# Three experts with one-hot rows instead of two, weights issued in one run behind the first gathers, page turns moved into the gating chain, a last tile copied by two engines, and a smaller first piece of x

## The chip, the cores and the metric

The kernel runs on one core of a Trainium2 chip. The core has a matmul engine (TensorE, called PE in the profile, with PEld for its weight loads), VectorE (DVE), ScalarE (ACT), GpSimd (POOL) and SyncE (SP). SP, ACT and POOL also issue DMAs, which run on 16 shared DMA engines. Each engine works through its own instructions in order. The metric is the time of one execution on the device in microseconds; the median of several runs counts.

## The reference

The program is a Fourier filter over the sequence, followed by a mixture of experts in which each expert keeps at most 80 tokens:

```python
X = np.fft.rfft(x, axis=1)                  # x: (8, 2496, 256)
y = np.fft.irfft(X * (filt_r + 1j * filt_i), n=2496, axis=1)
x = y.reshape(19968, 256)
logits = x @ w_gate                         # 8 experts
expert = argmax(logits); gate_w = softmax(logits)[expert]
for e in range(8):
    tok = tokens of expert e; at most 80, those with the largest gate_w
    out[tok] = gate_w[tok] * (relu(x[tok] @ w1[e]) @ w2[e])   # 256 -> 1024 -> 256
```

All other rows of the output are zero. So only 640 of the 19968 rows of the inverse transform are ever needed, and the kernel computes only chosen rows of it.

## The kernel before, in words

**Forward transform.** The sequence of 2496 is split as 39 by 64. For each of 16 halves (8 batches, two halves of 128 channels) `stage1` (line 316) multiplies x by a table, ScalarE copies the result, and for each of five groups of frequencies `turn_t` (332) transposes on PE, `stage2` (343) multiplies by the second table, and `filtered` (352) multiplies by the filter on VectorE (line 358) and adds and subtracts on POOL (366). One such group is a step k; the loop at line 1033 has 80 of them. x comes in three chunks per batch by `load_x` (288); the first chunks come in pieces of four rows (`SG`) for each partition.

**Filter.** The filter is read in five groups (`filter_in`, 532), the real part by SP and the imaginary part by POOL, each followed by a part of the second table on SP. `filter_sign` (542, VectorE) changes the sign of some of its rows in place; `filter_turn` (548) then brings a group into place with PE, by plain transposes where the sign has been applied, else by products with a table `perm`, in twice as many passes. There are ten such turns, one ahead of the loop and one in each of the steps 0 to 8. `perms` holds both tables and the signs. Ahead of the loop a row of eight products of zeros keeps PE at work until x lands (line 938).

**Gates.** The logits are found from the spectra, for two batches at a time: `gates` and `turn_z`, `logits`, and `gating` (466) in eleven parts, which leave the best eight candidates per row. For the last batch `gates_last` and `turn_z_last` do this in smaller pieces as the spectrum becomes ready. `threshold` (570) finds by bisection the gate value that keeps 80 tokens of each expert; `mark`, `codes`, `fields`, `row_lists`, `row_index` turn the kept tokens into row numbers.

**Chosen rows of the inverse transform.** The chosen tokens are sorted by batch into seven tiles of 128 rows (`TILES`). For each tile `gather_rows` (895, POOL) reads rows of a table of the inverse transform (640 numbers each), `turn_rows` (906, VectorE) transposes them, and `fill` (913) does the product with the spectrum of the batch, 20 steps per tile. A spectrum as it stands in memory is a page: `load_page` (872) reads it back on SP, and the last batch's page is made on the core by ten calls of `turn_last` (389), each four PE transposes and one ScalarE copy. A finished tile is copied by ScalarE (929) and written to `y_sel` in DRAM by a DMA that ScalarE issues (930).

**Experts.** For an expert its 80 tokens are gathered from `y_sel` by POOL (rows of 256 numbers), transposed (`turn`, 1244), and go through `layer1` (1259), `layer2` (1279), a transposition back (`back`, 1307) and an indirect write to the output (`scatter`, 1317). The first `NH` experts do not wait for the last tile to be written: `last_dg` and `last_hot` (806, 812) make a one-hot matrix `lhot` of the rows that lie in the last tile, the gather at line 1217 reads only the tiles before it, and `turn` adds a product of the last tile, still on the core, with `lhot`. The other experts gather from the whole of `y_sel` (line 1238) and wait for that DMA. `turn(e + 2)` stands between the two halves of `layer2(e)`.

**Weights.** Each expert has two DMAs on SP, `load_first` (w1, 1107) and `load_second` (w2, 1115). They go into places that pages or earlier experts have used: expert 2 takes the place of page 4, 3 that of page 5, 4 that of page 6, 5 to 7 those of experts 0 to 2. With a `mark`, POOL clears one number of the place first, so the DMA is held back until POOL gets there in its queue.

The order of the work on each engine is written out by hand (`tc.manual_schedule()`); from line 1125 on the calls stand in the order in which the engines take them.

## Time and profile before

| | |
|---|---|
| median of 3 runs | 373.41 us (373.08 to 377.3) |
| the profiled execution | 374.22 us |
| its span in the trace | 372.3 us |
| PE busy | 353.7 us, 95% of the span |
| PEld busy | 317.4 us, 85% |
| VectorE busy | 241.2 us, 65% |
| POOL busy | 189.7 us, 51% |
| ScalarE busy | 130.9 us, 35% |
| moved by DMA | 109.96 MB, mean 295 GB/s |

How to read the rows. In a timeline a row is the start, the length, the engine, the line of the kernel, the operation, output <- inputs with their shapes, and the count of instructions merged; in brackets stands the idle time of the engine ahead of it and what ended it. "SPq" and the like are the issuing of DMAs. A list of waits gives the engine and line that waited, what released it, and the sum in us, the number and the longest. In a table of stretches a row is the stretch, its length, the busy time of PE, PEld, DVE, ACT and POOL with the count of instructions, then the granted clock of PE (1.00 is full), the busy share of the DMA engines, and GB/s. A row of a group ends with its busy time, the mean of one in ns, and the idle time ahead of it. The chain of waits is the work that ended last, followed back; its rows are start, length and what. Matmuls are pipelined, so a matmul in f32 appears as passes that overlap, and the spacing of starts says more than the length of one.

### The profile page before, as it was taken

The page shows a single profiled execution, that of the slowest core. Times are in us where ns is not written, and L with a number is a line of the kernel's source. Part 1 is how long each engine was busy: PE and PEld are TensorE (multiplying, and loading weights), DVE is VectorE, ACT ScalarE, POOL GpSimd, SP SyncE. Part 2 cuts the span into 40 slices and gives each one's busy share as a digit, 9 for nine tenths or more (in the row PEclk, how much of TensorE's full clock was granted, in tenths as well). Part 3 has the DMA queues.
Part 4 walks back from the last instruction along what each step waited for, and adds up shares of the span by engine and source line. Part 5 has one row for each costly group of instructions (what it writes and reads, how often), then busy time and mean ns, then how long its engine had stood idle before and what let it go on. Part 6 is the DMA issues. An engine that isn't in the chain of part 4 may idle for free. (4 is left out here: it accounts for less than half of the span.)

```text
span 372.3 us, 9878 instructions
## 1 busy us (share of the span) xinstructions
PE 353.7 (95%) x4021; PEld 317.4 (85%) x4021; DVE 241.2 (65%) x514; ACT 130.9 (35%) x274; POOL 189.7 (51%) x273
## 2 busy tenths in 40 slices
PE   8989999999999999999899999989999999898893
PEld 7989989899899899799699979679886757787793
DVE  6089648748868768979979897688976660111120
ACT  1645454454455455354354444225000000010110
POOL 4688556646646646646457888712275102323111
PEclk9999999999999999999999999999999999899997
DMA  6997659999989999999989979988999966599900
GB/s 229 326 319 271 144 163 297 328 310 321 334 278 337 312 339 355 349 275 339 322 276 291 347 252 325 345 333 325 410 408 407 387 230 227 186 369 369 331 22 26
DMA packets 42235, 109.96 MB, mean 295 GB/s; under 512 B 4533, under 2 KB 14643, under 8 KB 40895
## 3 DMA queue, kind: packets, MB, share of 16 engines
q1 hardware_dynamic: 34708, 83.50, 65.0%
q0 software_dynamic: 6192, 24.60, 19.6%
q10 hardware_dynamic: 1282, 1.14, 1.0%
q8 instruction: 34, 0.56, 0.6%
q14 instruction: 19, 0.16, 0.1%
HBM read 70.44 MB, written 40.37 MB: 298 GB/s over the span
## 5 line engine op out<-in xcount | busy, mean ns | idle before, releaser
L366 POOL TENSOR_TENSOR yt<-p 128x256 f32<-128x256 f32 x159 | 116.5, 755 | 76.3 <-DVE p L358 75.2
L358 DVE TENSOR_TENSOR p<-pb,ft 128x1024 f32<-128x1024 f32 x80 | 97.1, 1215 | 41.9 <-issue 18.2
L323 PE MATMUL pa<-wf_t,x 117*128 117x120 f32 x704 | 92.0, 278 | 0.7 <-DMA x<-in_x_dram 0.7
L323 PEld LDWEIGHTS pa<-wf_t,x 117*128 117x128 f32 x704 | 86.5, 196 | 1.0 <-issue 1.0
L348 PE MATMUL pb<-d_t,t 128*128 128x128 f32 x640 | 84.9, 276 | 0.4 <-DVE p L358 0.3
L348 PEld LDWEIGHTS pb<-d_t,t 128*128 128x128 f32 x640 | 77.8, 192 | 0.9 <-issue 0.8
L328 ACT COPY tt<-pa 128x480 f32<-128x480 f32 x96 | 48.0, 516 | 69.3 <-PE pa L323 68.0
L341 ACT COPY t<-pt 128x512 f32<-128x512 f32 x80 | 47.1, 589 | 16.9 <-PE pt L337 13.8
L379 DVE STREAM_TRANSPOSE u<-yt 128x512 f32<-128x512 f32 x70 | 48.9, 699 | 0.0
L337 PE MATMUL pt<-ident,tt 128*128 128x128 f32 x320 | 48.4, 273 | 0.0
L901 POOL DMA_INDIRECT gt<-rows_tbl,idxr x28 | 29.5, 1053 | 27.3 <-DVE wt L911 19.1
L337 PEld LDWEIGHTS pt<-ident,tt 128*128 128x128 f32 x320 | 37.4, 142 | 1.1 <-issue 1.0
L920 PE MATMUL pr<-page,wt 128*128 128x256 f32 x160 | 36.8, 382 | 0.0
L920 PEld LDWEIGHTS pr<-page,wt 128*128 128x128 f32 x160 | 29.6, 190 | 4.2 <-issue 0.6
L925 PE MATMUL pr<-page,wt 128*32 128x256 f32 x480 | 27.5, 380 | 0.4 <-DVE wt L911 0.4
L911 DVE STREAM_TRANSPOSE wt<-gt 128x640 f32<-128x640 f32 x28 | 21.9, 819 | 5.8 <-DMA gt<-rows_tbl,idxr 5.8
L925 PEld LDWEIGHTS pr<-page,wt 128*32 128x32 f32 x480 | 17.2, 110 | 9.7 <-DVE wt L911 0.9
L1269 PE MATMUL ph_True<-xs_True,w 128*64 128x80 f32 x512 | 21.9, 242 | 2.9 <-issue 2.5
L1318 POOL DMA_INDIRECT out_dram<-ys_True,idxs x8 | 7.5, 932 | 31.6 <-ACT ys_True L1313 22.9
L1269 PEld LDWEIGHTS ph_True<-xs_True,w 128*64 128x64 f32 x512 | 20.2, 144 | 3.9 <-issue 3.8
L929 ACT COPY yr<-pr 128x256 f32<-128x256 f32 x7 | 2.6, 373 | 54.0 <-PE pr L925 28.5
L404 PE MATMUL pz<-yt,wg 128*32 128x512 f32 (+1 forms) x224 | 19.5, 437 | 1.7 <-POOL yt L366 1.7
(220 smaller groups left out, 316.0 us busy)
## 6 DMA issues: line engine op xcount, KB each, us to landing
out_dram<-zero_t SPq DMA_DIRECT2D x32, 624.0 KB
yf<-u SPq DMA_DIRECT2D x56, 320.0 KB
page<-yf SPq DMA_DIRECT2D x14, 1280.0 KB
w<-in_moe_w_dram SPq DMA_DIRECT2D x16, 1024.0 KB
x<-in_x_dram POOLq DMA_DIRECT2D x11, 936.0 KB
x<-in_x_dram SPq DMA_DIRECT2D x12, 468.0 KB
x<-in_x_dram POOLq DMA_DIRECT2D x5, 702.0 KB
fst<-in_filt_r_dram SPq DMA_DIRECT2D x10, 128.0 KB
```

Source lines behind the costliest of these rows:

```text
L323: nc.tensor.matmul(out=ps[:, j, :], rhs=wf_t, start=True, stop=True, lhsT=xt[3 * b + ch][:, j0 + j - JC * ch, 128 * cb:128 * cb + 128])
L328: nc.scalar.copy(out=tt[h][:, :, H3 * j0:H3 * j0 + hn * jn].rearrange("p s (j h) -> p s j h", h=hn), in_=v)
L337: nc.tensor.transpose(ps[:, i, :], tt[h][:, 2 * s:2 * s + 2, :].rearrange("p r n -> p (r n)"), ident[:])
L341: nc.scalar.copy(out=t2[k][:], in_=ps[:])
L348: nc.tensor.matmul(out=ps[:, :, i, :], lhsT=t[:, i, :], rhs=d_t[:, SG * g + i, :], start=True, stop=True)
L358: nc.vector.tensor_tensor(out=p[:], in1=f.unsqueeze(2).to_broadcast(shape), op=AL.mult, in0=ps[:].rearrange("p r s q -> p r (s q)").unsque ...
L366: eng.tensor_tensor(out=y[:, :, 2 * r:2 * r + 2, :], in0=a, in1=b, op=op)
L379: nc.vector.transpose(uu[h][:, :, SG * g:SG * g + SG, :].rearrange("p a s w -> p s a w"), spectrum(h)[:, SG * g:SG * g + SG])
L901: nc.gpsimd.indirect_dma_start(out=gts[t, g][:].rearrange("p s q -> p (s q)"), out_offset=None, in_=quarters, in_offset=bass.IndirectOffse ...
L920: nc.tensor.matmul(st["po"][:], lhsT=wts[t][:, s, :], rhs=columns(pages[t], s), **kw)
L925: nc.tensor.matmul(st["po"][at], lhsT=wts[t][:, s, at], rhs=columns(pages[source(t, g)[0]], s), **kw)
L1269: nc.tensor.matmul(ph[c:c + 64, i, 0:cap], lhsT=w1[:, k, f:f + 64], rhs=xs[:, k, :], start=(k == 0), stop=(k == NDB - 1))
```

## The change

There are five edits. **NH = 3**: a third expert gets one-hot rows; its one-hot product and the second's now stand between steps of the last tile. **Weights**: the second half for expert 3 and both halves for expert 4 are issued right behind those of expert 2, ahead of the last tile's end in the order of the program, and no longer behind the gathers of the other experts; the `mark` for expert 3's second half goes. **Turns**: three of the ten `turn_last` calls move up between the steps that lead to the last logits. **Last tile**: its two halves are copied by ScalarE and VectorE. **Start**: the first chunk of x comes as pieces of 2, 2 and 4 rows and not 4 and 4; ScalarE's DMA for `perms` moves behind the first pieces of stage 1; `filter_sign` moves behind `filtered` in the steps 0 to 4, group 2 (before: ahead of the loop) becomes the last of the five, and so group 2's first turn is by `perm`.

```diff
-NH = 2
+NH = 3
...
             elif i < 7:
-                for j in range(0, jn, SG):
-                    rows_in(0, [(N2, N1), (J3, H3)], r0 + j, min(SG, jn - j), j)
+                cuts = [0, 2, 4, jn] if i == 0 else list(range(0, jn, SG)) + [jn]
+                for j, end in zip(cuts, cuts[1:]):
+                    rows_in(0, [(N2, N1), (J3, H3)], r0 + j, end - j, j)
...
         def last_dg(e):
-            where, tag = ((sp, "bval"), (sp, "spread"))[e]
-            st["dg", e] = where.tile([cap, cap], F32, name=f"dg_{e}", tag=tag)
+            st["dg", e] = sp.tile([cap, cap], F32, name=f"dg_{e}",
+                                  tag=("bval", "spread", "part")[e])
...
-                    nc.scalar.copy(out=yr[:], in_=st["po"][:])
+                    if t < TILES - 1:
+                        nc.scalar.copy(out=yr[:], in_=st["po"][:])
+                    else:
+                        nc.scalar.copy(out=yr[:, 0:128], in_=st["po"][:, 0:128])
+                        nc.vector.tensor_copy(out=yr[:, 128:C], in_=st["po"][:, 128:C])
...
-        nc.scalar.dma_start(out=perms[:], in_=perm_dram.ap())
         for i in range(3):
             load_x(i)
...
         for i in range(4):
             for h in range(2):
                 stage1(h, i)
+            if i == 0:
+                nc.scalar.dma_start(out=perms[:], in_=perm_dram.ap())
...
         next_filter(nc.vector.tensor_copy)
-        filter_sign(2)
...
                 next_filter(nc.scalar.copy)
-                if r < NG - 1:
-                    filter_sign((r + 3) % NG)
...
                 filtered(k, ps)
+            if k < NG:
+                filter_sign((k + 3) % NG)
...
+        pages[B - 1] = keep.tile([128, NS * C], F32, name=f"page_{B - 1}", tag="page1")
         gates_last(2)
...
         gates_last(4)
+        turn_last(0)
         turn_z_last(0, 4)
         fill(1)
         turn_z_last(4, 1)
         gating(2, 8)
+        turn_last(1)
         logits(7, 0)
         for part in range(9, 11):
             gating(2, part)
         fill(1)
+        turn_last(2)
         logits(7, 1)
...
-        pages[B - 1] = keep.tile([128, NS * C], F32, name=f"page_{B - 1}", tag="page1")
         gating(3, 9)
         gating(3, 10)
         threshold(B, cap, 0)
-        for i in range(2 * NG):
+        for i in range(3, 2 * NG):
             turn_last(i)
...
-        last_dg(0)
-        last_dg(1)
+        for e in range(NH):
+            last_dg(e)
...
         last_hot(0)
-        last_hot(1)
         xg = [near_p.tile([cap, C], F32, name=f"xg_first_{e}") for e in range(NH)]
...
         load_first(2, nc.gpsimd.memset)
+        load_first(3)
         load_second(2)
-        load_first(3)
-        fill(20)
+        load_second(3)
+        for e in range(1, NH):
+            fill(2)
+            last_hot(e)
+        fill(22 - 2 * NH)
+        load_weights(4)
...
             gather(e)
-            if first and e == 4:
-                load_second(3, nc.gpsimd.memset)
-                load(4)
```

## The prediction

> **What bounds the kernel now.** I read the page's first lines, then what the matmul engine (PE) waits for, then the end of the run in order of time, where the largest of these waits lies, and last the granted clock in stretches of 2 us.
>
> ```profile
> span 372.3 us, 9878 instructions
> PE 353.7 (95%) x4021; PEld 317.4 (85%) x4021; DVE 241.2 (65%) x514; ACT 130.9 (35%) x274; POOL 189.7 (51%) x273
> ```
> ```profile
> PE ph_True L1269 <- issue: 2.5, 3, 1.1
> PE px_True L1254 <- DMA xg_True<-y_sel,idxg: 1.8, 1, 1.8
> ```
> PE is busy for 353.7 of 372.3 us. So 18.6 us are not covered by it, and an edit that gives PE no less work can win only part of these. The list has at its head three stops of 2.5 us together, named "issue", with no cause that the profile shows, and then one wait of 1.8 us for the gathered rows of an expert, which this change aims at. The waits below these two are short; those that the change touches stand in brackets in the rows further down.
>
> ```profile
> 313.30 0.45 PE L1249 MATMUL px_True<-ident,xg_first 80*128 80x80 f32 x2 [0.46 <-ACT yr L929]
> ...
> 314.26 0.39 PE L1249 MATMUL px_True<-ident,xg_first 80*128 80x80 f32 x2
> ...
> 319.72 1.28 PE L1287 MATMUL po_True<-hT_True,w 128*64 128x80 f32 x32
> ...
> 322.77 0.36 PE L1254 MATMUL px_True<-ident,xg_True 80*128 80x80 f32 x2 [1.77 <-DMA xg_True<-y_sel,idxg]
> ...
> 323.06 1.72 PE L1287 MATMUL po_True<-hT_True,w 128*64 128x80 f32 x32
> ...
> 328.22 0.41 PE L1310 MATMUL pb_True<-ident,yT_True 128*80 128x128 f32 x2
> ...
> 329.82 0.36 PE L1254 MATMUL px_True<-ident,xg_True 80*128 80x80 f32 x2
> ...
> 358.72 1.33 PE L1287 MATMUL po_True<-hT_True,w 128*64 128x80 f32 x32
> ...
> 359.87 2.40 PE L1269 MATMUL ph_True<-xs_True,w 128*64 128x80 f32 x64
> ...
> 362.20 0.42 PE L1310 MATMUL pb_True<-ident,yT_True 128*80 128x128 f32 x2
> ```
> ```profile
> 320.00:322.00 2.00, 1.00 (x30) 0.83 (x25) 0.43 (x1) 0.00 (x0) 1.51 (x2) 1.00 0.08 29
> 322.00:324.00 2.00, 1.23 (x28) 1.15 (x30) 0.21 (x1) 0.00 (x0) 1.48 (x3) 0.98 0.22 66
> 324.00:326.00 2.00, 2.00 (x34) 1.96 (x32) 0.44 (x2) 0.00 (x0) 0.00 (x0) 0.50 0.65 136
> 326.00:328.00 2.00, 2.00 (x44) 2.00 (x43) 0.00 (x0) 0.44 (x1) 0.00 (x0) 0.67 1.01 349
> ```
> This is the heart of the case. PE stops at 321.00 (319.72 + 1.28) for the rows of expert 2 and goes on at 322.77. Then the clock column (after the five engines) falls to 0.50 and 0.67: 1.00 + 0.66 + 0.04 = 1.7 us of PE time are lost in these stretches, after the wait and because of it, as nothing else there is odd. The same work late in the run shows full speed: the second half of a layer 2 takes 1.15 us (358.72 to 359.87) and a layer 1 takes 2.33 us (to 362.20).
>
> **The change, part by part.** *A third expert from one-hot rows (NH = 3).* Expert 2 no longer waits for the last tile's rows to go out and come back. Its rows are gathered behind those of experts 0 and 1, and its turn becomes the longer form, with two products for each half: 0.96 us (313.30 to 314.26) where the short form takes 0.29 (322.77 to 323.06). From 321.00: 0.96 for the turn, 1.15 for the half of layer 2, 2.33 for layer 1, so the next step starts at 325.44 and not at 328.22. That is **-2.8 us**, of which 1.7 is the clock and the rest the wait less 0.67 of added work. Lower end: if the clock is not cut in the timed runs, -1.1.
>
> What it adds ahead of the last tile:
>
> ```profile
> 303.36 0.45 PE L814 MATMUL pd<-dg,ones_f 80*128 80x80 f32 x2 [0.32 <-DVE bad L859]
> 313.28 6.12 DMA y_sel<-yr
> 274.71 8.19 DMA gt<-rows_tbl,idxr
> ```
> ```profile
> 308.46 0.97 POOL L1217 DMA_INDIRECT xg_first<-y_sel,idxg  x1 [0.30 <-issue]
> 309.43 0.11 POOL L1111 MEMSET w<- 128x1 f32 x1
> ...
> 320.18 0.96 POOL L1238 DMA_INDIRECT xg_True<-y_sel,idxg  x1 [10.64 <-PE ph_True L1269]
> ...
> ```
> ```profile
> 306.00:308.00 2.00, 2.00 (x44) 1.22 (x40) 0.00 (x0) 0.00 (x0) 0.82 (x1) 1.00 0.00 0
> ...
> 340.00:350.00 10.00, 9.29 (x212) 8.06 (x210) 1.96 (x5) 1.73 (x4) 1.90 (x2) 1.00 1.06 376
> ```
> One more product for the one-hot matrix on PE, up to 0.45 us at line 814. The second of these products now waits 0.3 us for VectorE; with two steps of the last tile between them that wait has other work, but the transposes that these need end at the same time, so I take **+0.2** (0 to 0.45). VectorE's extra clear, scaling and comparison come while PE has the last tile to do, from 303.8 to the first expert's turn at 313.30; without that cover they would cost under 1 us. On POOL's queue the third gather stands in front of the clear of the weight tile at 309.43; a gather takes 0.97 there and 0.3 to the next, so the clear moves to about 310.7.
>
> *Weights behind the first gathers.* SP now issues both halves for experts 2 and 3 in one go, and those of expert 4 as soon as the last tile's product frees their place; behind these its queue holds only expert 5's, which wait for PE's first layer 2 in any case. By their shapes three experts are 6.3 MB: at the 376 GB/s of the stretch 340 to 350 experts 2 to 4 end at about 327.5, and 5 to 7 at about 344. Expert 2's layer 1, at 323.1, needs only the first megabyte. DMA engines that stood at 0.00 in 306 to 308 and at 0.08 in 320 to 322 get work earlier; but in no row above does PE wait for weights, so this in itself brings **0**. On POOL a clear before expert 3's second half goes (0.11 us). What it collides with: the last tile's write (6.12 us) and the gathers of experts 3 and 4. Expert 3's starts at about 320.2, as expert 2's does now, and must have landed at turn 3, at 325.44 + 1.60 (328.22 to 329.82) = 327.0. It took 2.6 us for expert 2 in empty DMA engines (320.18 to 322.77); the worst gather in full ones took 8.19 with rows of 2.5 KB against 1 KB here. Between these I take 4 to 5 us, nearer the short one for its size: landed at 325, no wait. PE is busy for only 9.29 of 10 us in the stretch 340 to 350, where the DMA engines are full (1.06): if the stops named "issue" belong to that, moving the transfers forward may add or drop one of them, +-1.1 (the longest in the list). I take 0.
>
> *Last tile copied by two engines.* The wait of 0.46 us in the row at 313.30 is for this copy; half the width on each of two engines leaves some 0.3 to 0.4: **-0.1**.
>
> *Three turns of the last page into the gating chain.*
>
> ```profile
> 251.09 4.72 PE L393 MATMUL pq<-ident,yt 128*128 128x128 f32 x40
> ...
> 252.07 4.99 ACT L395 COPY page<-pq 128x512 f32<-128x512 f32 x10 [0.40 <-PE pq L393]
> ...
> 254.11 0.42 DVE L580 TENSOR_TENSOR spread<-row,thot 128x256 f32<-128x256 f32 x1
> ...
> 255.65 0.60 PE L590 MATMUL pall<-spread,same_f 128*128 128x256 f32 x2
> ...
> ```
> The ten turns hold PE for 4.72 us, and the product at line 590 starts behind them at 255.65, although its input is ready at 254.53. Seven turns take 3.3 us; so up to 1.1 can be won, and then VectorE's threshold is next. Against it: each turn also puts a ScalarE copy of 0.5 us (4.99 by 10) into the queue in front of the copies that carry the logits, and some of the three will delay VectorE's chain: 0 to 1.5. Ends: -1.1 and +0.4. I take **-0.5**, for PE has short gaps there that the turns fill.
>
> *The start: a smaller first x, the tables later, the signs later.*
>
> ```profile
> 0.74 5.36 SPq L297 DMA_DIRECT2D x<-in_x_dram  x6
> ...
> 1.10 3.78 PE L939 MATMUL warm<-z 128*128 128x128 f32 x16 [1.10 <-POOL z L133]
> ...
> 5.58 11.66 PE L323 MATMUL pa<-wf_t,x 117*128 117x120 f32 x84 [0.70 <-DMA x<-in_x_dram]
> ...
> 19.69 0.75 DVE L544 TENSOR_SCALAR fst<-fst,perm 128x1024 f32<-128x1024 f32 x1
> ...
> 21.08 2.37 POOL L886 MEMSET gt<- 128x640 f32 x4
> ...
> 21.61 2.40 DVE L544 TENSOR_SCALAR fst<-fst,perm 128x1024 f32<-128x1024 f32 x1 [1.16 <-DMA fst<-in_filt_r_dram]
> ...
> 24.10 0.63 PE L555 MATMUL pf<-perm,fst 128*128 128x128 f32 x4 [1.10 <-issue]
> ```
> ```profile
> L323 PE MATMUL pa<-wf_t,x 117*128 117x120 f32 x7 | 1.7, 421 | 0.0
> ```
> ```profile
> L323 PE MATMUL pa<-wf_t,x 117*128 117x120 f32 x11 | 1.4, 275 | 0.0
> ```
> PE's warm-up ends at 4.88 and x lets it go on at 5.58. Half the bytes, without the table beside them, close that gap: 0.7 at best. The same matmuls take 421 ns from 8 to 9 us (first fence of one row) and 275 from 11 to 12 (second): PE is slow at first. A cut that loses 1.7 us at the half clock of 324 to 326 lasts 3.4 us; if an unbroken run is let go that much earlier, 1.7 more are won. But all this ends at a later gate: the transposes of filter group 3 at 24.10, which idled 1.10, stand behind the sign operation at 21.61, which waited 1.16 for its filter to land, and that lands behind the same bytes as now. SP has one more x to issue in front of the filters (six took 5.36 us, so 0.9 later at worst, where the queue and not the engines is full). The operation took 2.40 beside POOL's clears, and 0.75 alone. So PE gets there between 22.4 and 24.1, with a gain of 0 to 1.7. I take **-0.9**. The sign of group 2 leaves the place before the first filtering and goes behind it, so the two products of group 2 become plain ones (four more passes, 0.6 us of PE by the row at 24.10), which lies in that wait. The perm table, issued behind ScalarE's first two copies, has until about 14.8 to land (17.24, the end of the row at 5.58, less the 2.4); if it is late, it costs what the start brings.
>
> Sum: -2.8 + 0.2 + 0 - 0.1 - 0.5 - 0.9 = -4.1. The profiled execution took 374.22 (span 372.3 and 1.9 around it), so 370.1. The median of the runs shown, 373.41, is 0.8 below it: **369.3**.
>
> **Rivals.** *The wait costs no clock.* If 1.77 us of idling don't cut the clock, in the timed runs at least, expert 2 brings 1.1 and not 2.8, and the sum is -2.4: 371.0. Against it: 0.50 follows the gap in the rows above. For it: this is one execution, and the timed runs are 0.8 us below it. Chance 0.2. The Trainium skill, page "TensorE: Matmul & The Clock Gate", section "HAM oscillation — how this bites in real kernels", puts the limit at idle gaps of more than about 3.4 us, by which a gap of 1.77 would cut nothing. By that rule the row at 324 should read 1.00; it reads 0.50, so the trace does not agree.
>
> *The start keeps all it wins.* If filter 3 lands earlier too, 0.7 + 1.7 = 2.4 in place of 0.9: -5.6, 367.8. For it: PE has the gap and the slow stretch. Against it: the filter's landing. Chance 0.12.
>
> *The wait comes back one expert later.* One mechanism: the rows of expert 3 are now read while the weights of 2 to 4 fill the DMA engines, where those of expert 2 were read from empty ones. If the gather takes the 8.19 of the worst row behind its issue (321.14), it lands at 329.3, 2.3 after turn 3 wants it; with a new clock cut of 1.7 the sum is about 0. If the write before it takes that long too (8.2 for 6.1), 2.1 more: 375.4. It decides from a landing at about 329.4 on. Against it: rows of 1 KB, not 2.5. Chance 0.08. The Trainium skill, page "DMA: Bandwidth & Descriptors", section "Queues, rings and completion order", says that a DMA engine takes turns between the queues that have work, packet by packet, so that a longer backlog on SP's queue would slow neither a write on ScalarE's nor a gather on POOL's. No row here has the same transfer beside two lengths of backlog.
>
> *The change does not do what it says.* The rows of expert 2 would have to land after 321; gathered third, at about 309.7, they have 11 us. Then the sum lacks the 2.8: 372.1. With the case that the moved turns only delay the logits (+0.4 in place of -0.5: 370.2) I give it 0.05.
>
> **How the numbers follow.** The forecast has 0.55: 369.3, its own ends 368 to 370.5. The range reaches to the clock rival and to most of the start rival with one stop of 1.1 on either side: 366.2 to 372.6; that leaves out the late gather, some of the start rival and the tails, not quite 2 in 10. 2% is 7.5 us, about what a measurement of this kernel tells from no change. Faster than 365.9 needs the full start, the full 1.1 of the turns and a stop fewer: 0.06. Slower than 380.9: 0.02. Within: 0.92.
>
> **What would show it.** Right: in the list of PE's waits the gather at line 1254 is gone, the clock stays at 1.00 from 320 to 330, layer 1 of expert 2 takes about 2.4 us, the product at line 590 starts behind seven turns and not ten, and PE's filter transposes still stop for a sign operation near 22 to 24. Wrong: a new wait of PE on the gather of expert 3, clock stretches below 1.00 after 320, a landing of the last tile's write well over 6 us, the logits of the last pair later than they are now against the last filtering, or a PE that passes filter group 3 before 22.

## The result

The kernel became slower, not faster. The median is 377.26 us (375.78 to 379.51, 18 runs) against 375.38 us (372.07 to 379.36, 18 runs) for the kernel before, timed beside it: a ratio of 1.0063 with a 95% interval of 1.0037 to 1.0089. By 2% that is no difference. Timed once more (f1 below) the ratio was 1.0067 (1.0041 to 1.0093). The forecast of 369.3 and its range to 372.6 both lie below it. In the group e5 to e8 below, nine of the 33 runs of the kernel before were over 1.5% above its quickest and are left out of the ratios.

The profiled execution took 378.18 us, its span 376.4. The page's first lines, and the head of the list of what TensorE (PE) waits for, of the changed kernel:

```profile
span 376.4 us, 9904 instructions
PE 355.1 (94%) x4033; PEld 316.0 (84%) x4033; DVE 240.9 (64%) x518; ACT 130.9 (35%) x274; POOL 190.0 (50%) x272
```
```profile
PE ph_True L1281 <- issue: 3.9, 3, 1.7
PE pa L324 <- DMA x<-in_x_dram: 3.1, 5, 1.2
PE pz L405 <- POOL yt L367: 1.7, 2, 1.4
PE pf L556 <- DVE fst L545: 1.7, 2, 1.3
```

The wait for an expert's gathered rows, 1.8 us before, is gone, as intended. Two things stand in its place: the stops named "issue" are 3.9 us instead of 2.5, and PE now waits 3.1 us for x at the start, where it waited 0.7.

The start of the changed kernel in order of time (start, busy us, engine, line, what; in brackets the idle time in front and who ended it):

```profile
4.68 0.66 PE L324 MATMUL pa<-wf_t,x 117*128 117x120 f32 x4
6.21 1.60 PE L324 MATMUL pa<-wf_t,x 117*128 117x120 f32 x12 [0.87 <-DMA x<-in_x_dram]
9.02 2.04 PE L324 MATMUL pa<-wf_t,x 117*128 117x120 f32 x16 [1.20 <-DMA x<-in_x_dram]
...
17.20 1.57 PE L324 MATMUL pa<-wf_t,x 117*128 117x120 f32 x12 [0.30 <-DMA x<-in_x_dram]
...
27.13 0.63 PE L556 MATMUL pf<-perm,fst 128*128 128x128 f32 x4 [1.28 <-DVE fst L545]
```

PE begins 0.9 us earlier (4.68 for 5.58; for this gap the forecast had 0.7 at best). But then each new piece of x finds it waiting. PE's own pace is not what holds it: in the trace its passes of stage 1 start 0.11 us apart from 6.5 us on, where before they started 0.21 apart until 10 us. The transposes of filter group 3 start at 27.13 and not at 24.10, because the sign operation in front of them gets its filter later. It began at 21.61 before, and now:

```profile
26.04 0.99 DVE L545 TENSOR_SCALAR fst<-fst,perm 128x1024 f32<-128x1024 f32 x1 [1.15 <-DMA fst<-in_filt_r_dram]
```

From there to the end of the main loop the changed kernel is 3.3 us late; the loop, bound by PE, neither makes this up nor adds to it.

The last tile and the first expert, in the same view, and the granted clock (behind the five engines' busy times) where it had fallen to 0.50 before:

```profile
309.55 1.07 PE L926 MATMUL pr<-page,wt 128*32 128x256 f32 x16
310.55 0.45 PE L815 MATMUL pd<-dg,ones_f 80*128 80x80 f32 x2
310.93 5.21 PE L926 MATMUL pr<-page,wt 128*32 128x256 f32 x77
316.45 3.23 PE L926 MATMUL pr<-page,wt 128*32 128x256 f32 x51 [0.32 <-issue]
319.61 0.45 PE L1261 MATMUL px_True<-ident,xg_first 80*128 80x80 f32 x2
```
```profile
324.00:326.00 2.00, 2.00 (x64) 2.00 (x62) 0.49 (x1) 0.44 (x1) 0.00 (x0) 1.00 1.08 384
326.00:328.00 2.00, 2.00 (x49) 1.91 (x46) 0.49 (x1) 0.00 (x0) 0.95 (x1) 1.00 1.10 372
```

The same view of the kernel before, its last tile:

```profile
303.74 9.10 PE L925 MATMUL pr<-page,wt 128*32 128x256 f32 x160
```

The clock stays at 1.00. But the 160 passes that ran without a break in 9.10 us before now last until 319.68, with one-hot products between them and stops between 314.4 and 316.5: 77 passes, which at the old pace (9.10 by 160) are 4.4 us, are spread over 5.21, and then PE stands still for 0.32.

To compare executions I cut them at four marks: the 41st transpose step of the main loop ("step 41" below; line 338 of the changed kernel), the "misc" product ahead of the last tile (line 858), the first layer-1 product of the experts (line 1281) and the end. In the two profiled executions, in us:

| stretch | before | after | difference | forecast |
|---|---|---|---|---|
| start to step 41 of the loop | 122.74 | 126.04 | +3.30 | -0.9 |
| to "misc" (the gating chain is in it) | 179.84 | 181.23 | +1.39 | -0.5 |
| the last tile, to the experts' first layer 1 | 12.66 | 14.49 | +1.83 | +0.1 |
| experts to the end | 57.09 | 54.61 | -2.48 | -2.8 |
| sum | 372.33 | 376.37 | +4.04 | -4.1 |

So the part that was largest in the forecast came, and everything around it went the other way. Of the +1.39, 0.4 lies ahead of the product at line 591 and 1.0 behind it; 0.6 of that comes with one stop of the weight loads, at 297.6, which no other execution shows. What of this is the change and what the chance of two executions, the experiments say.

### The profile page after: what moved, and what is told of

It reads as the page before. It is cut to its first block, busy times and chain, and to the rows that moved or that the text cites. A ratio compares the mean times of both kernels' runs of the same rounds, so it can differ in the third digit from the quotient of the medians.

```text
span 376.4 us, 9904 instructions
## 1 busy us (share of the span) xinstructions
PE 355.1 (94%) x4033; PEld 316.0 (84%) x4033; DVE 240.9 (64%) x518; ACT 130.9 (35%) x274; POOL 190.0 (50%) x272
## 4 chain that ended last, share of the span: by engine, by line
PE 51%; issue 15%; POOL 10%; DVE 10%; DMA 9%; SPq 2%; ACT 1%; POOLq 1%; DVEq 0%
PE pb L349 14%; PE pa L324 14%; PE pt L338 7%; PE pr L926 5%; POOL yt L367 4%; PE pz L405 4%; DMA x<-in_x_dram 3%; POOL gt L902 2%; DMA gt<-rows_tbl,idxr 2%; DVE p L359 2%; POOL out_dram L1330 2%; DMA fst<-in_filt_r_dram 2%; DMA y_sel<-yr 2%; DVE wt L912 1%; SPq L297 1%
## 5 line engine op out<-in xcount | busy, mean ns | idle before, releaser
L324 PEld LDWEIGHTS pa<-wf_t,x 117*128 117x128 f32 x704 | 85.0, 192 | 4.1 <-DMA x<-in_x_dram 2.4
L342 ACT COPY t<-pt 128x512 f32<-128x512 f32 x80 | 47.1, 589 | 16.9 <-PE pt L338 14.9
L926 PE MATMUL pr<-page,wt 128*32 128x256 f32 x480 | 29.9, 381 | 1.2 <-DVE wt L912 0.5
L1281 PE MATMUL ph_True<-xs_True,w 128*64 128x80 f32 x512 | 19.8, 233 | 3.9 <-issue 3.9
L1281 PEld LDWEIGHTS ph_True<-xs_True,w 128*64 128x64 f32 x512 | 18.7, 137 | 4.5 <-issue 4.3
L1299 PE MATMUL po_True<-hT_True,w 128*64 128x80 f32 x448 | 18.5, 235 | 0.0
```

The costliest lines, as they stand in the source:

```text
L324: nc.tensor.matmul(out=ps[:, j, :], rhs=wf_t, start=True, stop=True, lhsT=xt[3 * b + ch][:, j0 + j - JC * ch, 128 * cb:128 * cb + 128])
L342: nc.scalar.copy(out=t2[k][:], in_=ps[:])
L926: nc.tensor.matmul(st["po"][at], lhsT=wts[t][:, s, at], rhs=columns(pages[source(t, g)[0]], s), **kw)
L1281: nc.tensor.matmul(ph[c:c + 64, i, 0:cap], lhsT=w1[:, k, f:f + 64], rhs=xs[:, k, :], start=(k == 0), stop=(k == NDB - 1))
```

## The experiments

Each kernel was timed against the kernel before on its chip (median and ratio with 95% interval). The runs came in five groups: e1 to e4, e5 to e8, e9 to e12, f1 to f4 and g1 with g2. The last two groups fell on the same chip, the others each on another.

**The parts, one by one.** *e1_start: the three edits of the start alone.*

```diff
-                for j in range(0, jn, SG):
-                    rows_in(0, [(N2, N1), (J3, H3)], r0 + j, min(SG, jn - j), j)
+                cuts = [0, 2, 4, jn] if i == 0 else list(range(0, jn, SG)) + [jn]
+                for j, end in zip(cuts, cuts[1:]):
+                    rows_in(0, [(N2, N1), (J3, H3)], r0 + j, end - j, j)
...
-        nc.scalar.dma_start(out=perms[:], in_=perm_dram.ap())
         for i in range(3):
...
+            if i == 0:
+                nc.scalar.dma_start(out=perms[:], in_=perm_dram.ap())
...
-        filter_sign(2)
...
-                if r < NG - 1:
-                    filter_sign((r + 3) % NG)
...
+            if k < NG:
+                filter_sign((k + 3) % NG)
```


> Only the three edits of the start (x in pieces of 2, 2 and 4 rows, the perm table behind the first pieces of stage 1, the signs behind the filtering). Theory A, from the two traces: the 3.3 us by which every step from the second batch on is late in the changed kernel are made by these edits, because x and the filters land later; then this kernel is 2.5 to 3.5 us slower than before, with waits of PE for x of about 3 us and the filter transposes at 27 us and not at 24. Theory B: the late start is an accident of the one profiled execution; then it lies within 0.7 us of before.

376.45 us, ratio 1.0032 (1.0006 to 1.0058): 1.2 us slower, between the two theories. In its trace PE waits 1.3 us for x, and the transposes of filter group 3 start at 25.61; theory A said 3 and 27. The start edits cost time, but not the 3.3 us of the profiled pair.

*e2_tail: the third expert, the two-engine copy and the new weight order, nothing else.*

```diff
-NH = 2
+NH = 3
...
-        last_hot(1)
...
+        load_first(3)
         load_second(2)
-        load_first(3)
-        fill(20)
+        load_second(3)
+        for e in range(1, NH):
+            fill(2)
+            last_hot(e)
+        fill(22 - 2 * NH)
+        load_weights(4)
...
```


> Only the third expert with one-hot rows, the order of the weights, and the last tile copied by two engines. Theory A: it wins what the forecast said for the experts (2.8 us less 0.2) minus some 1.2 us that the last tile lost in the changed kernel: 1 to 2.5 us faster than before. Theory B, under which the loss of the changed kernel lies here: 1 to 2 us slower. In the trace the granted clock stays at 1.00 from the first expert on.

375.31 us, ratio 0.9998 (0.9973 to 1.0024); timed again as e12_tail_again, 1.0001 (0.9961 to 1.004). Nothing of the 2.7 us arrives.

*e3_turns: the three turns in the gating chain alone* (the lines with `turn_last` and `page_` of the diff above), *and e4_turns_tail: the changed kernel without its start edits.*

> Only the three turns of the last page moved into the gating chain. By the trace of the changed kernel the product at the head of the threshold search comes 0.4 us later against the steps before it: Theory A 0.3 to 0.6 us slower than before. The forecast's own value was 0.5 us faster.

> The changed kernel without the edits of the start. Theory A: 0.5 to 2 us faster than before, and 2.5 to 3.5 us faster than the changed kernel. Theory B: within 0.7 us of the changed kernel, so about 2 us slower than before.

e3: 374.74 us, 0.9988 (0.9961 to 1.0015). e4: 375.59 us, 1.0001 (0.9973 to 1.0029). The turns bring nothing that can be measured, and without the start edits the changed kernel is as fast as the one before.

**The start, edit by edit.** *e9_xcut, e10_perms and e11_sign are the three pieces of e1's diff, each alone.*

> The smaller first piece of the first x alone. In eight executions with the old start the 41st stage step of the main loop began 122.3 to 125.3 us into the span, 124.0 on average; in the two with all three start edits at 124.7 and 126.0, and those edits together took 1.2 us of time. Theory S1 (the cut is the cost: more issues and smaller packets while TensorE waits for x): 0.9 to 1.5 us above before here, that step at 124.7 us or later, and nothing in e10_perms and e11_sign. Theory S2 (the cut helps by itself, since TensorE starts 0.9 us sooner, and the cost is in the other two): 0.3 to 0.9 us below before.

> The load of perms moved behind the first x's stage alone. Theory S1 (the cut of x costs): within 0.4 us of before. Theory S3 (perms comes later into the time in which the queues are full, and the filter's products wait for it): about 1.2 us above before, the first filter products later than 20 us into the span (16.3 to 19.4 us in executions with the old start).

> The sign of the filter groups moved into the main loop's first steps alone. Theory S1: within 0.4 us of before. Theory S4 (the sign, now behind the loop's copies on its engine, comes late for the products of the first steps): about 1.2 us above before, and the fourth stage step at 27 us or later where the first one is not late (24.2 to 26.8 us with the old start).

e9: 376.08 us, 1.0025 (0.9989 to 1.006). e10: 375.95 us, 1.0018 (0.9984 to 1.0051). e11: 374.07 us, 0.9975 (0.9939 to 1.001). Each interval holds 1, so the three alone settle nothing. Step 41 stands at 124.31 in e9, a little before the 124.7 that S1 asked for, but the order of the three fits S1. The next pair tells more. *f1_after_again is the changed kernel; f2_no_xcut is the same with this undone:*

```diff
-                cuts = [0, 2, 4, jn] if i == 0 else list(range(0, jn, SG)) + [jn]
-                for j, end in zip(cuts, cuts[1:]):
-                    rows_in(0, [(N2, N1), (J3, H3)], r0 + j, end - j, j)
+                for j in range(0, jn, SG):
+                    rows_in(0, [(N2, N1), (J3, H3)], r0 + j, min(SG, jn - j), j)
```


> The changed kernel once more, beside the next three. Theory S1 (the cut of x costs) and theory D or E (the last tile's stop) both put it at 1.003 to 1.009 of before where the stop is there (12 us or more from the misc product to the experts' first matmul), and at 0.999 to 1.003 where it is not.

> The changed kernel with the first x in its old pieces; all its other edits stay. Theory S1 (the cut costs): 0.9 to 1.5 us below f1_after_again. Theory S2 (the cut is free and the other start edits cost): equal to f1_after_again within 0.4 us.

f1: 376.75 us, 1.0067 (1.0041 to 1.0093). f2: 375.49 us, 1.0023 (0.999 to 1.0056). The cut of the first x costs 376.75 - 375.49 = 1.3 us, the 0.9 to 1.5 of theory S1; the two half-widths, 0.0026 and 0.0033, give the difference of 0.0044 an uncertainty of about 0.0042, so it is just clear of zero. It shows in the ten microseconds behind the first issues. The stretch 4 to 14 us (busy time of PE, its weight loads, VectorE, ScalarE and POOL, then clock, share of the 16 DMA engines, GB/s), f1 with the cut and then f2 without:

```profile
4.00:14.00 10.00, 7.83 (x61) 7.00 (x60) 3.16 (x28) 4.54 (x7) 1.20 (x3) 1.00 0.90 239
```
```profile
4.00:14.00 10.00, 9.13 (x62) 8.86 (x61) 3.16 (x28) 4.63 (x7) 2.50 (x5) 1.00 0.92 280
```
```profile
0.74 6.20 SPq L297 DMA_DIRECT2D x<-in_x_dram  x7
13.00 0.18 POOL L946 COPY fst<-x 1x1 f32<-1x1 f32 x1 [8.49 <-DMA x<-in_x_dram]
```
```profile
0.74 5.36 SPq L297 DMA_DIRECT2D x<-in_x_dram  x6
11.70 0.18 POOL L945 COPY fst<-x 1x1 f32<-1x1 f32 x1 [7.19 <-DMA x<-in_x_dram]
```

With the cut the DMA engines move 239 GB/s, without it 280. That PE is busy for 7.83 us of the 10 with it and 9.13 without does not mean less work: the passes are 61 and 62, but f2's start 0.21 us apart until 9.7 us and f1's 0.11 apart, with waits for x between them (the 1.00 in f2's row hides this: its trace has no record of the clock before 9.6 us). SP needs 6.20 us for seven issues and 5.36 for six. The small POOL copy, which waits for a later x to land, runs at 13.00 instead of 11.70: 1.3 us later, the size of the price.

Why the rate is lower is open. The share of busy time of the DMA engines hardly differs (0.90 and 0.92). The 2 KB packets of the small pieces took 101 ns each from 4 to 9 us, about half of the 187 that a 4 KB packet took in f2, but the 4 KB packets beside and behind them took 224 in f1. The later issue, 0.84 us, is at most a part.

In the four executions with the cut the rate was 239 to 263 GB/s, mean 250; in the sixteen without, 255 to 314, mean 282. On each chip with both kinds the kernels with the cut had the lowest rate. But the same start too differs, by up to a fifth on one chip (264 and 314 in e2 and e3), and step 41 of the loop with it: 122.3 to 125.3 us in sixteen executions without the cut, 123.8 on average (124.3 to 126.0 and 125.0 in the four with it; 124.99 and 124.59 in f1 and f2). The kernel before was profiled in one of its quickest starts. By these means about 2 of the 3.3 us of the table are that chance, and 1.1 to 1.3 are the cut.

**The third expert: why it brings nothing.** *e5_hots_first is e2_tail with the three one-hot products ahead of the last tile's matmuls.*

```diff
-        last_hot(0)
+        for e in range(NH):
+            last_hot(e)
...
-        for e in range(1, NH):
-            fill(2)
-            last_hot(e)
-        fill(22 - 2 * NH)
+        fill(20)
         load_weights(4)
```
*e6_no_gather3 is e2_tail without the third gather; the third expert's rows stay zero.*

```diff
             nc.vector.memset(xg[e][:], 0.0)
+            if e == 2:
+                continue
             nc.gpsimd.indirect_dma_start(
```
*e7_third_old is e2_tail with the old weight order, and e8_weights the new weight order with two experts as before.*

> The third expert's rows and the new weight order (as in e2_tail), but the three one-hot products stand back to back ahead of the last tile's matmuls, as the two stood before; the two-engine copy is kept. From the misc product to the first matmul of the experts the kernels with two experts took 10.2 to 10.7 us and those with three 12.1 to 12.8. Theory A (the one-hot products between the matmuls break the last tile): the stop of 1.3 to 1.5 us in the last tile is gone, that stretch is 10.8 to 11.2 us, and the time is 1 to 1.5 us below before. Theory B (the third gather stops TensorE): the stop stays, the stretch is 12 us or more, and the time is that of before within 0.5 us.

> As e2_tail, but the third expert's gather is left out, so that its rows stay zero and its tokens come out wrong; everything else stays, its one-hot product too. Theory A (products between the matmuls): the stop of 1.3 to 1.5 us stays, and the time is within 0.5 us of e2_tail. Theory B (the third gather stops TensorE): no stop, the stretch from the misc product to the experts' first matmul falls from 12.8 to about 11.3 us, and the time is 1.2 to 1.5 us below before.

> The third expert's rows with the weights in the order of before (the second matrix of the fourth expert and the fifth expert's weights are issued behind the gathers of the experts' loop). Theory A or B (the stop comes from the products or from the third gather): the stop is there as in e2_tail, the last tile's stretch 12 us or more, time within 0.5 us of before. Theory C (the new weight order makes the stop, by SP's issues and transfers beside the last tile): no stop, stretch about 11.3 us, and the time 1 us or more below before.

> Two experts' rows as before, with the new weight order alone: the weights are issued straight behind the first gathers. Theory A or B: no stop in the last tile (10.2 to 10.8 us from the misc product to the experts' first matmul), and the time is that of before within 0.5 us, since the experts wait for no weights in either order. Theory C (the order makes the stop): a stop of 1.3 us or more in the last tile and a time about 1.3 us above before.

e5: 371.85 us, 0.9976 (0.9945 to 1.0006). e6: 372.23 us, 0.9985 (0.9951 to 1.0018). e7: 371.8 us, 0.9962 (0.9932 to 0.9991). e8: 375.78 us, 1.0074 (1.0042 to 1.0106). On this chip none of the four stopped in the last tile, so A, B and C could not be told apart by it. What the group did show is the cost of the weight order with two experts, which no theory had. The wait for the rows of the third expert (index 2) in e8, and the clock behind it:

```profile
319.05 0.96 POOL L1240 DMA_INDIRECT xg_True<-y_sel,idxg  x1 [10.06 <-PE ph_True L1271]
325.96 0.53 PE L1256 MATMUL px_True<-ident,xg_True 80*128 80x80 f32 x2 [6.06 <-DMA xg_True<-y_sel,idxg]
```
```profile
326.00:328.00 2.00, 2.00 (x26) 1.83 (x28) 0.32 (x1) 0.00 (x0) 0.00 (x0) 0.50 1.08 325
```
```profile
321.39 0.96 POOL L1239 DMA_INDIRECT xg_True<-y_sel,idxg  x1 [10.61 <-PE ph_True L1270]
324.04 0.36 PE L1255 MATMUL px_True<-ident,xg_True 80*128 80x80 f32 x2 [2.06 <-DMA xg_True<-y_sel,idxg]
```

The gather is issued at 319.05 and its rows are used at 325.96, 6.9 us later, while the weights issued in front of it keep the DMA engines full (a share of 0.99 to 1.12 in all stretches of 2 us from 312 to 326); with the old order (e10, last fence) 2.65 us are enough, in engines that stand at 0.14 from 322 to 324. The new order is harmless only together with a third expert whose rows are read before the weights start. That is the rival "the wait comes back one expert later" in its mechanism, one expert earlier.

*e12_tail_again and f3_third_old_again repeat e2 and e7 on chips that do stop; f4_sign_third is f3 with the sign of e11.*

> The kernel of e2_tail once more. The three kernels that have the third gather, the one-hot products between the matmuls and the new weight order (e2_tail, e4_turns_tail and the changed kernel) stopped for 1.3 to 1.5 us in the last tile, those with any of the three undone did not (e5_hots_first, e6_no_gather3, e7_third_old), but ran in another session. Theory D (the three together make the stop): the stop is there again, 12 us or more from the misc product to the experts' first matmul, time within 0.5 us of before. Theory E (the stop belongs to the session, not to the code): no stop, 11.5 us, and a time 0.9 to 1.4 us below before, as in e7_third_old.

> The kernel of e7_third_old once more, beside the changed kernel. Theory C (the new weight order makes the stop in the last tile, and the old order leaves it out): 1 us or more below before, no stop of over 1 us. Theory E (the stop belongs to the chip): where the changed kernel stops in the last tile, this one does too, and its time is within 0.5 us of before; where the changed kernel does not stop, this one is 1 us or more below before.

> The third expert's rows with the old weight order and the two-engine copy, and the sign moved into the loop; the start's other edits, the turns and the new weight order are left out. If the parts add (0.9962 or 1.0001 for the third expert, 0.9975 for the sign): 0.9 to 2.3 us below before. If the sign's 0.25% was chance: equal to f3_third_old_again within 0.5 us.

e12: 375.2 us, 1.0001, with 1.40 us from one weight load to the next at one place of the last tile (some 0.06 elsewhere). f3: 374.14 us, 1.001 (0.9979 to 1.004), with two such places, of 0.51 and 0.67, so the old order does not take the stop away and theory C falls. f4: 373.72 us, 0.9978 (0.9947 to 1.0008): not clear of zero. No version is shown to beat the kernel before on a chip with the stop.

*g1_no_gather3 and g2_hots_first are e6 and e5 once more, one run each, on the chip of f1 to f4.*

> The kernel of e6_no_gather3 once more: the third gather is left out, so the third expert's rows stay zero and its tokens come out wrong. Theory B (the third gather stops TensorE): no stop of 1 us or more in the last tile, 11.5 us from the misc product to the experts' first matmul. Theory A (the products between the matmuls): a stop of 1.1 to 1.5 us, 12.3 us or more.

> The kernel of e5_hots_first once more: three gathers, the three one-hot products ahead of the last tile's matmuls. Theory B (the third gather): a stop of 1.1 to 1.5 us stays, 12.2 us or more from the misc product to the experts' first matmul. Theory A (the products between the matmuls): no stop, 11.1 us.

372.79 us and 374.25 us, one run each. The last tile's matmuls in g1, in g2, and in e5, which is g2 on the chip without the stop:

```profile
306.93 7.25 PE L925 MATMUL pr<-page,wt 128*32 128x256 f32 x128
```
```profile
305.26 9.99 PE L925 MATMUL pr<-page,wt 128*32 128x256 f32 x160
305.26 5.76 PEld L925 LDWEIGHTS pr<-page,wt 128*32 128x32 f32 x111
311.39 0.17 PEld L925 LDWEIGHTS pr<-page,wt 128*32 128x32 f32 x5 [0.36 <-issue]
312.11 0.18 PEld L925 LDWEIGHTS pr<-page,wt 128*32 128x32 f32 x6 [0.55 <-issue]
312.84 1.93 PEld L925 LDWEIGHTS pr<-page,wt 128*32 128x32 f32 x38 [0.55 <-issue]
...
311.21 0.96 POOL L1221 DMA_INDIRECT xg_first<-y_sel,idxg  x1 [0.30 <-issue]
```
```profile
303.67 8.84 PE L925 MATMUL pr<-page,wt 128*32 128x256 f32 x160
```

Without the third gather, 128 passes run through in 7.25 us, the products standing between the matmuls as before: theory A falls. With the gather and the products moved away, 160 passes take 9.99 us against 8.84 on the other chip, and the weight loads (PEld) come in small bunches with 0.36 to 0.55 us of nothing between them, from 311.0 to 312.8, about where the third gather is issued (311.21). So the long stop, about 1.1 us in g2, goes with the third gather; g1 is one execution, but all nine with three gathers outside the chip of e5 to e8 have the stop, and the two on that chip do not.

That the third gather alone is to blame is not shown. In the changed kernel, f1 and g2 the stop begins 0.2 to 0.3 us before the row of the third gather, where the second ends. And of the nine executions with two gathers, four (e3, e9, e10, e11) have one shorter stop right behind the second: 0.25 to 0.56 us from one weight load to the next. The longest, in e9:

```profile
310.94 0.97 POOL L1218 DMA_INDIRECT xg_first<-y_sel,idxg  x1 [0.30 <-issue]
312.48 1.94 PEld L926 LDWEIGHTS pr<-page,wt 128*32 128x32 f32 x40 [0.45 <-issue]
```

What the gathers take from TensorE I can't say: the DMA engines stand at 0.27 and 0.39 there (310 to 314, g2), and no engine or semaphore is named in the profile. That stays open.

## Why the prediction was wrong

The sign was wrong: -1.1% forecast, +0.6% measured. Two steps failed. The start was put at -0.9 and cost 1.2 us in e1. The third expert with the last tile was put at -2.8 + 0.2 - 0.1 = -2.7 and brought nothing in e2 and e12. The timed parts e1, e2 and e3 add up to +0.7 us where the whole change measured +2.4, a difference that their intervals allow and that no experiment divides further. By the prediction's own steps:

**The start, -0.9: this step failed.** Its ends were 0 and -1.7, with no loss. The bound was argued from what lands last (filter group 3) "behind the same bytes as now", and the one sentence on SP's extra issue, "0.9 later at worst", was set aside. The bytes are the same, but with the cut they flow more slowly, some 32 GB/s less on average from 4 to 14 us; the x behind them lands 1.3 us later (f1 against f2), and the start costs 1.2 us by the timed runs, 2.1 off the forecast. PE's slow first stretch, worth up to 1.7 in the forecast, did end earlier in the changed kernel and f1, and that brought nothing, since PE then waits for x. That the filter's group is a gate was right: PE's transposes still stop for it, at 27.13, and in the profiled pair its sign operation starts 4.4 us later (26.04 for 21.61).

**The turns in the gating chain, -0.5, ends -1.1 and +0.4: the bad end.** The lines of after that answer to the prediction's, and then the one of before from which the chain is counted:

```profile
254.63 0.52 PE L517 MATMUL pk<-ident,key 128*128 128x128 f32 x3 [0.24 <-DVE key L512]
254.98 1.03 PE L921 MATMUL pr<-page,wt 128*128 128x256 f32 x4
255.85 3.25 PE L394 MATMUL pq<-ident,yt 128*128 128x128 f32 x28
259.34 0.70 PE L591 MATMUL pall<-spread,same_f 128*128 128x256 f32 x2 [0.24 <-DVE n L586]
```
```profile
249.84 0.55 PE L516 MATMUL pk<-ident,key 128*128 128x128 f32 x3 [0.41 <-DVE key L511]
```

Seven turns take 3.25 us instead of 4.72, and the product at line 591 stands behind VectorE now: from the keys' transposes (254.63) to it are 4.7 us, where 5.8 were (249.84 to 255.65). These 1.1 us are won. But from the 80th step of the loop to the keys' transposes it takes 19.4 us (235.23 to 254.63) and not 17.9 (231.93 to 249.84): the turns in front delay the logits by 1.5. In this pair the net is +0.4. But the kernel before was a quick draw here too. From the 80th step to the product the five executions with the turns take 24.0 to 24.1 us, and the eleven without them, those on the chip of e5 to e8 left out, 23.6 to 24.6, mean 24.1: what the turns win at the product they lose ahead of the keys. From the product to "misc" they take 47.1 to 47.9 us where all the others take 46.5 to 46.9, which no experiment explains. e3's timing, 0.9988, holds a gain of 0.5 as well as a loss.

**The third expert, -2.8: the mechanism was right, its clock part mostly an accident, and the price in the last tile was missed.** Experts to the end took 2.48 us less in the profiled pair. But 1.7 of the 2.8 was a clock cut. Of seven executions with two experts, in which PE waited for these rows, three have the cut, those with waits of 1.77, 1.92 (e11) and 6.06 us (e8); in four it stays at 1.00, after waits of 2.06, 2.06, 2.24 and 2.98 us. The longest of these, e3, and its clock:

```profile
323.83 0.36 PE L1257 MATMUL px_True<-ident,xg_True 80*128 80x80 f32 x2 [2.98 <-DMA xg_True<-y_sel,idxg]
```
```profile
324.00:326.00 2.00, 2.00 (x56) 1.91 (x57) 0.65 (x2) 0.00 (x0) 0.80 (x2) 1.00 0.33 84
326.00:328.00 2.00, 2.00 (x52) 1.72 (x50) 0.24 (x1) 0.44 (x1) 0.00 (x0) 1.00 0.83 230
```

So the rival "the wait costs no clock", which had 0.2, holds in four of six executions with the old weight order. The rule of the Trainium skill, page "TensorE: Matmul & The Clock Gate", section "HAM oscillation — how this bites in real kernels", by which only idle gaps above about 3.4 us cut the clock, fits these four and e8 and fails in the two others: 1.77 us cut the clock and 2.98 did not, so by these runs the length of the gap alone doesn't decide.

What does is where the gap falls. A cut lasts 3.41 us, or 6.83 in e8, and within one execution the recorded changes of the clock are whole multiples of 3.41 us apart (12 and 92 in before). On that grid of 3.41 us, these are the stretches around the gap in before (cut at 323.91) and e11 (cut at 324.56), and the two that share the gap of e3 (no cut); the first number behind the length is PE's busy time:

```profile
320.50:323.91 3.41, 1.64 (x42) 1.39 (x38) 0.12 (x1) 0.00 (x0) 2.68 (x4) 1.00 0.17 52
```
```profile
321.15:324.56 3.41, 1.49 (x42) 1.33 (x36) 0.49 (x1) 0.00 (x0) 2.11 (x3) 1.00 0.19 62
```
```profile
318.74:322.15 3.41, 2.11 (x62) 1.95 (x58) 0.49 (x1) 0.38 (x1) 0.94 (x1) 1.00 0.63 255
322.15:325.56 3.41, 1.73 (x44) 1.65 (x46) 0.34 (x2) 0.00 (x0) 2.04 (x4) 1.00 0.25 62
```

In all twenty traces, from 20 us on, a cut begins, or goes on, at the end of each stretch of the grid in which PE was busy for less than half (1.64 us of 3.41 or less), and none begins behind one with 1.72 or more. The grid lies differently in each execution, so a gap of 1.8 to 3 us costs the clock or not by chance.

The cut is also cheaper than 1.7: the experts take 57.0 us with it (before and e11) and 56.1 without (e1, e9, e10), at waits 0.3 longer, so 1.2, or 1.0 if e3 is counted too.

Against this stands the last tile. "+0.2" for it was far too little: with two experts it took 12.4 to 12.7 us in all seven executions, with a third one 13.07 (e5, products in front) to 13.5 (e6, e7 and g1, products between) without a stop, and 13.7 to 14.8 with it. So the products and what waits for them are worth 0.5 to 1.0 (0.2 of it is the two-engine copy, below), and the stop that goes with the third gather 0.2 to 1.3 more. On the chip without the stop the third expert did bring time (e7, 0.9962); on the others the last tile ate it.

**Weights behind the gathers, 0: not shown to be 0.** The stops named "issue" in the experts were taken as +-1.1. In ten executions with the third expert and the new order (two of them without its gather) they are 3.0 to 4.4 us, mean 3.7; in nine with the old order 2.5 to 4.1, mean 2.9; but e8, the new order with two experts, has 1.2. By the traces each such stop of over 0.3 us ends 2.3 to 2.7 us behind the start of a 16 KB transfer of instructions, mostly at times when the DMA engines are full, as the new order makes them earlier. That this is the cause is only argued. From the first layer 1 to the end the third expert took 55.0 us with the new order (mean of ten) and 54.3 with the old (three): 0.6 us, within what executions differ by.

**The late gather** (0.08) did not come: expert 3's rows are there in time. Its price was near where its condition was met: 6.9 us from issue to use in e8, for 8.19. The prediction cited the page "DMA: Bandwidth & Descriptors" of the Trainium skill, section "Queues, rings and completion order", for engines that take turns between queues packet by packet, and drew from it that a longer backlog on SP's queue would slow no gather on POOL's. No run has the gather beside two lengths of backlog. But e8 and e10 have it beside a long one and beside an almost idle set of engines, and it takes 6.9 and 2.65 us. It did not wait out the backlog (the engines stayed full to about 328.5), which agrees with packets in turn, but sharing the engines cost it 4.3 us.

**The two-engine copy, -0.1,** is right only beside the turns. In the profiled pair it is 0.36 us from the last pass's end to the first one-hot product (319.68 to 320.04), and was 0.75 (312.84 to 313.59). From the last tile's last weight load to the first layer 1 it is 2.7 us in the four executions with the copy and the turns, and 2.8 in e3, which has the turns alone. Without the turns it is 3.2 to 3.3 with the two-engine copy (nine executions) and 3.0 to 3.1 with the old one (six): there it costs 0.2. The copies do not run side by side, as ScalarE's row and VectorE's show in the changed kernel:

```profile
319.72 0.27 ACT L933 COPY yr<-pr 128x128 f32<-128x128 f32 x1 [11.92 <-PE pr L926]
```
```profile
320.02 0.29 DVE L934 COPY yr<-pr 128x128 f32<-128x128 f32 x1 [8.68 <-ACT yr L933]
```

Without the turns PE's first weight load for the experts waits for the second copy (g1), where it waited for the single one (e10):

```profile
314.86 0.30 PEld L1259 LDWEIGHTS px_True<-ident,xg_first 80*128 80x128 f32 x2 [1.16 <-DVE yr L933]
```
```profile
314.28 0.30 PEld L1250 LDWEIGHTS px_True<-ident,xg_first 80*128 80x128 f32 x2 [0.94 <-ACT yr L929]
```

**The range** was too narrow on one ground: it took one profiled execution as the kernel's own. The median of the runs of before alone went from 373.41 (three) to 375.38 (eighteen), 2 us, more than any term of the sum but one. Its start was among the quickest of sixteen, and its clock cut came in two of six.

## What to carry to other kernels

Cutting a first load into smaller pieces started the engine sooner here, but everything behind it landed later: where the loop behind is bound by that engine, look at when the last piece lands, not the first. A wait that is taken out by work ahead of it must be charged with that work's whole price, including what its gathers do to TensorE. An idle gap of about 2 us cost the clock in some executions and not in others. Before a term is built on one stop or one clock reading, see whether it is in more than one execution.

## What the runs showed of the hardware

With three row gathers one behind the other on POOL's queue, TensorE's weight loads stop for about 1 us in all (1.15 us in g2 against e5), on three chips and not on a fourth; with two gathers four of nine executions show one stop of 0.25 to 0.56 us there. No cause is named in the profile.

In all twenty traces, from 20 us on, the clock is cut to 0.50 behind a stretch of 3.41 us, on a grid that is fixed within an execution, in which PE was busy for less than half (1.64 us and less; not 1.72 and more). So gaps of 1.77 and 1.92 us cut it and gaps of 2.06 to 2.98 did not.

The DMA rate in the first microseconds of one and the same code differs by more than a fifth between executions (255 to 314 GB/s in 4 to 14 us).
